# Transposing u by vector-engine block transposes and SBUF-to-SBUF copies in place of TensorE transposes

## The chip, the cores and the metric

One core of a Trainium2 chip. Times are microseconds of device time for one execution; the kernel before was timed three times. PE is TensorE, DVE VectorE, ACT ScalarE, POOL GpSimd and SP SyncE. DMAs issued from POOL go through the software queue, those from SP and ACT through hardware queues.

## The reference

A causal sliding-window attention (window 64) feeds a mixer block. B = 8, H = 8, S = 576, D = 64, so the model width is 512 and there are 4608 tokens.

```python
scores = scale * q @ k^T                  # masked to 0 <= i - j < 64
attn   = softmax(scores)                  # sum + 1e-9 in the denominator
x      = (attn @ v) as [B, S, H * D]
h      = x^T @ U @ V                      # rank 32, along the sequence
u      = x + h^T
out    = u + relu(u @ w_ch1) @ w_ch2      # 512 -> 2048 -> 512
```

## The kernel before

All matmuls are in bf16 and accumulate in f32. The weights are loaded once: `w1b` (512x2048) and `w2b` (2048x512).

The mixer's two large matmuls run over nine chunks of 512 tokens. The attention runs over eight batches of 576 tokens, so the borders of the two don't agree: tokens are counted in tiles of 128, `g` = 0 to 35, and chunk c is tiles 4c to 4c+3. Batch 0's attention is done ahead of everything (the prologue). From then on **stage c** is the mixer of chunk c with the attention of batch c+1 put in between its matmuls.

A stage has 32 slots. Slots 0 to 15 are `ch1(i)`: four matmuls of 512 columns into one bank (`psA`, L513) and a relu of it into `c1[i]`, on DVE for i = 1, 4, 7, 10, 13 and otherwise on ACT. Slots 16 to 31 are `ch2(t, quarter)`: four matmuls into `psU` (L535); after the fourth quarter DVE adds `u` (`osb`, L544) and SP stores the tile. `psA` and `psU` take turns in three banks of the pool `mm`. The loop at L655 runs each slot's matmuls and then the pieces of attention that the tables `PLACE`, `PLACE_1` (batch 1) and `PLACE_2` (batch 2) put behind that slot. The order of each engine's work is the order in which this loop writes it; every engine runs its own in that order.

The pieces of a batch b, with the engine that works longest in each:

- `KT` (L228): DVE transposes q and k in 32x32 blocks, from the loaded `kr`, `qr` into `kt`, `qt`. The KT of batch b+1 stands in the stage of batch b. For batches 0 to 2 ("paired") it moves pairs of bf16 as uint32, four instructions; from batch 3 on eight instructions of bf16.
- `S` (`SC`, L317): six pieces of scores on PE, exp on ACT (`pts`), the mask on DVE.
- `VC` (L263): DVE copies `vA` into `vB`, where the rows of v are shifted by 64.
- `PV` (L364): five tiles of attn @ v on PE, then a reciprocal and a multiplication on DVE, giving `xs`.
- `U` (L395): five matmuls into `pshh`, one copy on ACT (`hh`).
- `V` (L413): h^T on PE (`psv`) and the addition on DVE that gives `u` (`un`, one buffer for each tile g), for tiles (0,1), (2,3) and (4) of the batch.
- `UT` (L441): four PE transposes of a `u` tile by the identity (`tpu` or `tpw`, L451) and one copy out of PSUM (L456) into `uTc`, the operand of `psA`. Chunk 0 has another way (`XT` and `UP`, L469 and L481): x and h are multiplied by the identity and by V so that u comes out transposed.

`psA` contracts over the width in four parts of 128: part dc holds the features 128 dc to 128 dc + 127, of `uTc` and `w1b` alike.

Loads of q, k and v are all issued by POOL, in order. `load_kq(b)` fills `kr`, `qr` number b % 2. From batch 3 on it takes eight DMAs, one for each of four parts of k and of q in turn (k, q, k, q, ...), and loads each element twice, at two shifts. `load_v(b)` takes four DMAs into `vA` and one into `vB`, buffer b % 2. In stage c with b = c+1 the loop first issues `load_v(b + 1)` and, for b > 2, `load_kq(b + 2)`; in stage 1 `load_kq(4)` follows after slot 5, and in stage 0 `load_kq(2)` stands at the start and `load_kq(3)` after slot 23. They start as soon as their buffers are free.

Of the kernel before, what the change touches and what calls it, by code (L numbers as in the profile page):

```python
# [8 lines left out]
ACT = mybir.ActivationFunctionType  # L9
ALU = mybir.AluOpType  # L10

BF16 = mybir.dt.bfloat16
FP32 = mybir.dt.float32
# [3 lines left out]
def kernel(  # L17
# [43 lines left out]
    u_pool = ctx.enter_context(tc.tile_pool(name="un", bufs=14))  # L61
    c1_pool = ctx.enter_context(tc.tile_pool(name="c1", bufs=1))
    wk_pool = ctx.enter_context(tc.tile_pool(name="wk", bufs=2))
    out_pool = ctx.enter_context(tc.tile_pool(name="osb", bufs=4))
    ps_big = ctx.enter_context(tc.tile_pool(name="ps_big", bufs=2, space=bass.MemoryType.PSUM))
    first = ExitStack()
# [8 lines left out]
    NT = 5  # L75
    ident = const.tile([P, P], BF16, name="ident")
    mask = const.tile([P, 2 * NB, W], BF16, name="mask")
    w1b = const.tile([P, NDC, F], BF16, name="w1b")
    w2b = const.tile([P, NFC, DM], BF16, name="w2b")
    ub = [const.tile([P, NT, R], BF16, name=f"ub{i}") for i in range(2)]  # L80
    vrep = const.tile([P, W + S + W], BF16, name="vrep")
    bias = const.tile([P, 12, W], BF16, name="bias")
    idle = const.tile([P, CH], BF16, name="idle")
    xs = [const.tile([P, NT, H, D], BF16, name=f"xs{i}") for i in range(2)]
    vA = [const.tile([P, NFULL, H, VW], BF16, name=f"vA{i}") for i in range(2)]
# [102 lines left out]
    )  # L188
    nc.vector.tensor_copy(out=bias[:, NB:12, :], in_=bias[:, 6:NB, :])

    w1v = moe_w_ch1.rearrange("(c p) n -> p c n", p=P)
    w2v = moe_w_ch2.rearrange("(i p) m -> p i m", p=P)

    def load_w1(lo, hi):
        nc.gpsimd.dma_start(out=w1b[:, :, lo:hi], in_=w1v[:, :, lo:hi])

    def load_w2(lo, hi):
        nc.gpsimd.dma_start(out=w2b[:, lo:hi, :], in_=w2v[:, lo:hi, :])
# [11 lines left out]
    u_tiles = {}  # L210
    uT_tiles = {}

    def uT_of(c):
        if c not in uT_tiles:
            uT_tiles[c] = uT_pool.tile([P, NDC, CH], BF16, name="uTc")
        return uT_tiles[c]


    def attention(b, alone=False):
# [221 lines left out]
        def UT(t):  # L441
            def f():
                g = g0 + t
                wide = b == 1 and t % 2 == 1
                if wide:
                    tpb = ps_big.tile([P, 2, 2 * CH], BF16, name="tpw", tag="big")
                    tp = tpb[:, 0, 0:CH].rearrange("p (c q) -> p c q", q=P)
                else:
                    tp = psum["tp"].tile([P, NDC, P], BF16, name="tpu", tag="tp")
                for dc in range(NDC):  # L450
                    nc.tensor.transpose(  # L451
                        tp[:, dc, :], u_tiles[g][:, dc * P : (dc + 1) * P], ident[:]
                    )
                col = (g % TPC) * P
                copy = dve_copy if wide else nc.scalar.copy
                copy(out=uT_of(g // TPC)[:, :, col : col + P], in_=tp[:])  # L456
            return f

        pcs["KT"] = [KT(x, n) for n in range(NJ if pair else NJJ) for x in "kq"]
# [9 lines left out]
        def XT(t):  # L469
            def f():  # L470
                for dc in range(NDC):
                    nc.tensor.matmul(
                        xT0[dc // 2][:, dc % 2, t * P : (t + 1) * P],
                        x[:, t, 2 * dc : 2 * dc + 2, :].rearrange("p h d -> p (h d)"),
                        ident[:],
                        start=(t == 0),
                        stop=False,
                    )
            return f

        def UP():  # L481
            for dc in (0, 2, 1, 3):
                nc.tensor.matmul(
                    xT0[dc // 2][:, dc % 2, :],
                    hh["sb"][:, dc * P : (dc + 1) * P],
                    vrep[:, W : W + CH],
                    start=False,
                    stop=True,
                )
            for dc in (0, 2, 1, 3):  # L490
                copy = dve_copy if dc // 2 else nc.scalar.copy
                copy(out=uT_of(0)[:, dc, :], in_=xT0[dc // 2][:, dc % 2, :])  # L492

        pcs["XT"] = [XT(t) for t in range(NFULL)]
        pcs["UP"] = UP
        pcs["PV"] = [PV(t) for t in range(NT)]
        pcs["U"] = [UM((t,)) for t in range(NT)] if alone else [UM(tuple(range(NT)))]
        pcs["V"] = [VM((0, 1)), VM((2, 3)), VM((4,))]
        pcs["UT"] = [UT(t) for t in range(NT if odd else NT - 1)]
        return pcs  # L500


    DVE_RELU = (1, 4, 7, 10, 13)

    def mlp(c):
        uTc = uT_of(c)
        c1 = [None] * NFC

        def ch1(i):
            def f():  # L510
                ps = psum["mm"].tile([P, CH], FP32, name="psA", tag="mm")
                for dc in (0, 2, 1, 3) if c == 0 else range(NDC):
                    nc.tensor.matmul(  # L513
                        ps[:],
                        w1b[:, dc, i * P : (i + 1) * P],
                        uTc[:, dc, :],
                        start=(dc == 0),
                        stop=(dc == NDC - 1),
                    )
                c1[i] = c1_pool.tile([P, CH], BF16, name=f"c1_{i}")  # L520
                if i in DVE_RELU:
                    nc.vector.tensor_relu(out=c1[i][:], in_=ps[:])  # L522
                else:
                    nc.scalar.activation(out=c1[i][:], in_=ps[:], func=ACT.Relu)  # L524
            return f

        acc = {}

        def ch2(t, quarter):
            def f():  # L530
                g = c * TPC + t
                if quarter == 0:
                    acc[t] = psum["mm"].tile([P, DM], FP32, name="psU", tag="mm")
                for i in range(4 * quarter, 4 * quarter + 4):
                    nc.tensor.matmul(  # L535
                        acc[t][:],
                        c1[i][:, t * P : (t + 1) * P],
                        w2b[:, i, :],
                        start=(i == 0),
                        stop=(i == NFC - 1),  # L540
                    )
                if quarter == 3:
                    osb = out_pool.tile([P, DM], FP32, name="osb")
                    nc.vector.tensor_tensor(  # L544
                        out=osb[:], in0=acc[t][:], in1=u_tiles[g][:], op=ALU.add
                    )
                    nc.sync.dma_start(out=outf[g * P : (g + 1) * P, :], in_=osb[:])
            return f

        order = [(t, r) for t in range(TPC) for r in range(4)]  # L550
        if c == 0:
            order = [(t, r) for r in range(4) for t in range(3)] + [(3, r) for r in range(4)]
        return [ch1(i) for i in range(NFC)] + [ch2(t, r) for t, r in order]


    PLACE = {
        "VC": [0],
        "S": [1, 1, 4, 4, 7, 7],
        "PV": [10, 10, 13, 13, 15],
        "KT": [8, 9, 11, 12, 14, 15, 16, 18],  # L560
        "U": [17],
        "V": [19, 20, 22],
        "UT": [21, 22, 23, 24, 25],
    }
    PLACE_1 = {
        "KT": [13, 14, 15, 16],
        "S": [16, 16, 18, 18, 20, 20],
        "VC": [21],
        "PV": [23, 23, 25, 25, 26],
        "U": [28],  # L570
        "V": [29, 30, 31],
        "UT": [30, 31, 31, 32, 32],
    }
    PLACE_2 = {
        "KT": [1, 2, 3, 4],
        "S": [5, 5, 8, 8, 11, 11],
        "VC": [9],
        "PV": [14, 14, 16, 16, 18],
        "U": [20],
        "V": [22, 23, 24],  # L580
        "UT": [24, 25, 26, 27, 28],
    }
    KT_3 = [19, 20, 21, 23, 25, 27, 29, 30]
    KT_4 = [11, 12, 14, 16, 18, 19, 22, 25]


    def turn_over(n, cols=CH, to=None):
# [67 lines left out]
    for c in range(NCH):  # L655
        slots = [[] for _ in range(NSLOT + 1)]

        def place(b, parts, where):
            if b not in att:
                att[b] = attention(b)  # L660
            for part in parts:
                for f, s in zip(att[b][part], where[part]):
                    slots[s].append(f)

        b = c + 1
        if b == 1:
            for f, n in zip(att[0]["V"], (6, 8, 10)):
                slots[n].append(f)
        if b < B:
            if b == 1:  # L670
                load_kq(2)
            if b + 1 < B:
                load_v(b + 1)
            if b + 2 < B and b > 2:
                load_kq(b + 2)
            if b == 2:
                slots[5].append(lambda: load_kq(4))
            if b == 1:
                slots[23].append(lambda: load_kq(3))
            where = {1: PLACE_1, 2: PLACE_2}.get(b, PLACE)  # L680
            if b <= 2:
                place(b, ("KT",), where)
            place(b, ("VC", "S", "PV"), where)
            if 3 <= b + 1 < B:
                place(b + 1, ("KT",), {2: {"KT": KT_3}, 3: {"KT": KT_4}}.get(b, PLACE))
            place(b, ("U", "V", "UT"), where)
        for fill, extra in zip(mlp(c) + [lambda: None], slots):
            fill()
            for f in extra:
                f()  # L690
# [30 lines left out]
```

## Time and profile before

| | us |
|---|---|
| median of 3 runs (329.2 to 330.07) | 329.75 |
| the profiled execution | 330.28 |
| its span, first to last instruction | 328.6 |
| prologue, up to the first psA | 23.8 |
| stage 0, up to the first psA of stage 1 at 63.74 | 39.9 |
| stages 1 to 6, each | 33.98 to 34.80 |
| stage 7, without attention | 27.8 |
| stage 8, without attention, to the end of the span | 31.5 |
| busy in 132.8 to 166.8 (stage 3): PE, DVE, ACT, POOL | 34.0, 23.3, 13.7, 10.8 |

The groups of instructions that the change touches (each line: line, engine, operation, tiles, shape, count, then busy us, mean ns of one, idle us of the engine before them and what ended it):

```profile
L513 PE MATMUL psA<-uTc,w1b 128*128 128x512 bf16 x576 | 131.4, 379 | 0.9 <-DVE uTc L492 0.6
L456 ACT COPY uTc<-tpu 128x512 bf16<-128x512 bf16 x30 | 17.6, 586 | 40.3 <-PE tpu L451 40.3
L431 DVE TENSOR_TENSOR un<-psv,xs 128x512 bf16<-128x512 f32 (+1 forms) x40 | 25.7, 682 | 7.0 <-PE psv L420 6.8
```

The time of a psA matmul, 379 ns, is from its start to its modelled end; in stage 7, 64 of them follow each other in 13.81 us, one every 216 ns, so the sum of busy times is more than the time they take. ACT's 40 us before `uTc` are idle time of an engine with little to do at that point, not a cost. The granted TensorE clock was full (0.998) throughout.

The DMA rows of the page (busy share in 40 slices of 8.2 us, in tenths; and what was moved):

```profile
DMA  7999999999999997999991911001100010021011
GB/s 120 156 199 209 206 137 173 206 197 141 170 189 180 181 111 96 203 105 63 176 225 13 73 64 67 1 2 55 75 2 0 34 66 30 2 89 39 2 64 64
```

The DMA engines are at work almost all the time up to about 175 us, then in short stretches: by 190 us the last loads have landed and only outputs are left.

### The profile page before, as it was taken

How to read it: one execution, taken by the hardware profiler on the slowest of the kernel's cores; microseconds unless marked ns; L12 is line 12 of the kernel's file. 1: busy time of each engine (PE TensorE's matmuls, PEld its weight loads, DVE VectorE, ACT ScalarE, POOL GpSimd, SP SyncE). 2: the span in 40 equal slices, each digit the busy share in tenths (PEclk: the TensorE clock that was granted, in tenths of full speed). 3: DMA queues.
4: the chain of work that ended last, by engine and by line, in shares of the span. 5: the costliest groups of instructions: out<-in, count | busy, mean ns of one | idle time of the engine just before them, and what ended most of it. 6: DMA issues, size and time to landing. Idle time of an engine off the chain costs nothing.

```text
span 328.6 us, 6914 instructions
## 1 busy us (share of the span) xinstructions
PE 318.5 (97%) x2949; PEld 156.3 (48%) x2949; DVE 195.1 (59%) x339; ACT 118.3 (36%) x188; POOL 83.0 (25%) x112
## 2 busy tenths in 40 slices
PE   8989989899999999999999999999999999999995
PEld 8544444454454545454544454445445444444442
DVE  7654759588787885689457955696456512212211
ACT  1524350365027423552246233732182224203400
POOL 8571419554626226125501400000000000000000
PEclk9999999999999999999999999999999999999999
DMA  7999999999999997999991911001100010021011
GB/s 120 156 199 209 206 137 173 206 197 141 170 189 180 181 111 96 203 105 63 176 225 13 73 64 67 1 2 55 75 2 0 34 66 30 2 89 39 2 64 64
DMA packets 96573, 34.34 MB, mean 105 GB/s; under 512 B 86688, under 2 KB 89888, under 8 KB 96544
## 3 DMA queue, kind: packets, MB, share of 16 engines
q0 software_dynamic: 91360, 24.48, 83.8%
q1 hardware_dynamic: 5184, 9.44, 8.3%
q8 instruction: 23, 0.38, 0.5%
q14 instruction: 6, 0.05, 0.1%
HBM read 48.94 MB, written 9.44 MB: 178 GB/s over the span
## 4 chain that ended last, share of the span: by engine, by line
PE 79%; DMA 12%; DVE 5%; POOL 2%; issue 1%; ACT 0%; DVEq 0%
PE psU L535 36%; PE psA L513 32%; DMA vA<-in_v_dram 7%; DMA kr<-in_k_dram 5%; PE xr L375 3%; PE sc L341 3%; PE psv L420 2%; PE tpu L451 2%; PE pshh L401 1%; DVE un L431 1%; POOL vA L124 1%; DVE xs L385 1%; DVE kt L243 0%; DVE qt L243 0%; DVE osb L544 0%
## 5 line engine op out<-in xcount | busy, mean ns | idle before, releaser
L535 PE MATMUL psU<-w2b,c 128*128 128x512 bf16 x576 | 135.1, 379 | 0.0
L513 PE MATMUL psA<-uTc,w1b 128*128 128x512 bf16 x576 | 131.4, 379 | 0.9 <-DVE uTc L492 0.6
L524 ACT ACTIVATE c<-psA 128x512 bf16<-128x512 f32 x99 | 59.3, 599 | 100.2 <-PE psA L513 99.6
L513 PEld LDWEIGHTS <-w1b 128*128 128x128 bf16 x576 | 53.9, 98 | 63.9 <-issue 1.7
L535 PEld LDWEIGHTS <-c 128*128 128x128 bf16 x576 | 53.6, 98 | 60.2 <-issue 3.0
L544 DVE TENSOR_TENSOR osb<-psU,un 128x512 f32<-128x512 f32 x36 | 24.8, 690 | 64.0 <-PE psU L535 63.9
L522 DVE TENSOR_SCALAR c<-psA 128x512 bf16<-128x512 f32 x45 | 30.8, 685 | 34.8 <-PE psA L513 34.6
L124 POOL DMA_DIRECT2D vA<-in_v_dram x32 | 28.4, 892 | 62.2 <-PE xr L375 19.8
L349 ACT ACTIVATE pts<-sc 128x768 bf16<-128x768 f32 x42 | 31.8, 808 | 11.8 <-PE sc L341 10.0
L456 ACT COPY uTc<-tpu 128x512 bf16<-128x512 bf16 x30 | 17.6, 586 | 40.3 <-PE tpu L451 40.3
L356 DVE TENSOR_TENSOR pts<-pts,mask 128x768 bf16<-128x768 bf16 x42 | 23.1, 557 | 12.2 <-ACT pts L349 9.3
L431 DVE TENSOR_TENSOR un<-psv,xs 128x512 bf16<-128x512 f32 (+1 forms) x40 | 25.7, 682 | 7.0 <-PE psv L420 6.8
L385 DVE TENSOR_TENSOR xs<-xr,rcp 128x512 bf16<-128x512 f32 (+1 forms) x40 | 27.6, 691 | 1.4
L112 POOL DMA_DIRECT2D kr<-in_k_dram x20 | 16.6, 828 | 21.8 <-DVE kt L243 8.8
L375 PEld LDWEIGHTS <-pts 128*64 128x64 bf16 x576 | 12.4, 110 | 10.4 <-DVE xs L385 5.2
L112 POOL DMA_DIRECT2D qr<-in_q_dram x20 | 16.5, 826 | 3.0 <-DMA vA<-in_v_dram 1.1
L243 DVE STREAM_TRANSPOSE kt<-kr 128x576 bf16<-128x576 bf16 x20 | 16.0, 799 | 0.0
L243 DVE STREAM_TRANSPOSE qt<-qr 128x576 bf16<-128x576 bf16 x20 | 15.7, 787 | 0.0
L375 PE MATMUL xr<-vB,pts 128*64 128x65 bf16 x320 | 15.4, 196 | 0.3 <-DVE vB L137 0.2
L341 PEld LDWEIGHTS <-kt 64*64 64x64 bf16 (+1 forms) x720 | 10.1, 105 | 10.8 <-issue 10.4
L410 ACT CAST hh<-pshh 128x512 bf16<-128x512 f32 x8 | 4.7, 586 | 28.9 <-PE pshh L401 28.9
L341 PE MATMUL sc<-qt,kt 64*64 64x128 bf16 (+3 forms) x720 | 12.9, 215 | 1.8 <-issue 1.4
(64 smaller groups left out, 161.8 us busy)
## 6 DMA issues: line engine op xcount, KB each, us to landing
out_dram<-osb SPq DMA_DIRECT2D x36, 256.0 KB, 2.0
kr<-in_k_dram POOLq DMA_DIRECT2D x26, 288.0 KB, 10.4
qr<-in_q_dram POOLq DMA_DIRECT2D x26, 288.0 KB, 11.4
vA<-in_v_dram POOLq DMA_DIRECT2D x32, 128.0 KB, 7.2
w2b<-in_moe_w_ch_dram POOLq DMA_DIRECT2D x2, 1024.0 KB, 19.2
w1b<-in_moe_w_ch_dram POOLq DMA_DIRECT2D x2, 512.0 KB, 9.6
w1b<-in_moe_w_ch_dram POOLq DMA_DIRECT2D x1, 1024.0 KB, 10.6
vB<-in_v_dram POOLq DMA_DIRECT2D x8, 64.0 KB, 7.8
```

The costliest lines, as they stand in the source:

```text
L112: nc.gpsimd.dma_start(out=dst[32 * part : 32 * (part + 1), off : off + NJJ * RD].rearrange("p (n x) -> p n x", x=r * D), in_=src[b, m * NJ ...
L124: nc.gpsimd.dma_start(out=va[:, t, :, 0:D], in_=v[b, :, t * P : (t + 1) * P, :].rearrange("h p d -> p h d"),)
L243: nc.vector.transpose(out=dst[:, n * S : (n + 1) * S].rearrange("q (m p e) -> q m e p", p=32, e=r), in_=src[:, 32 + n * RD : 32 + (n + 1) ...
L341: nc.tensor.matmul(sc[half * W : (half + 1) * W, g, (a - lo) * W : (z - lo) * W], operand("k", g, jj, e, kb * W, (kb + 1) * W), operand("q ...
L349: nc.scalar.activation(out=dst, in_=sc[:, :, 0 : PB * W].rearrange("p g (n w) -> p g n w", w=W), func=ACT.Exp, scale=scale,)
L375: nc.tensor.matmul(xr[r0 : r0 + W, h // 4, (h % 4) * VW : (h % 4 + 1) * VW], pts[:, g, jj * NB + blk, :], rhs, start=True, stop=True,)
L385: nc.vector.tensor_tensor(out=x[lo:hi, t, :, :].rearrange("p (a h) d -> p a h d", a=2), in0=xv[:, :, :, 0:D], in1=rcp[lo:hi].to_broadcast( ...
L431: nc.vector.tensor_tensor(out=u_tiles[g][rs, :], in0=ps[rs, n, :], in1=xt[n][rs], op=ALU.add)
L513: nc.tensor.matmul(ps[:], w1b[:, dc, i * P : (i + 1) * P], uTc[:, dc, :], start=(dc == 0), stop=(dc == NDC - 1),)
L522: nc.vector.tensor_relu(out=c1[i][:], in_=ps[:])
L524: nc.scalar.activation(out=c1[i][:], in_=ps[:], func=ACT.Relu)
L535: nc.tensor.matmul(acc[t][:], c1[i][:, t * P : (t + 1) * P], w2b[:, i, :], start=(i == 0), stop=(i == NFC - 1),)
```

## The change

1. For chunks 2 to 8 the `UT` pieces are gone. In their place `TR(g)` transposes a `u` tile on DVE in 32x32 blocks of uint32, that is of pairs of neighbouring features, into a staging tile `stg` (two buffers), and `gather(c)` moves the blocks of the four tiles to their partitions with 16 DMAs inside SBUF, in turn from ACT and SP. Each moves 32 partitions of 1 KB in runs of 512 B. Chunk 1 keeps its `UT`, chunk 0 its own way.
2. So that pairs can stay together, the four parts of the contraction are now (g, e): features 256 g + 2 p + e on partition p. `w1b` is loaded in that order (each load as two DMAs), `uTc` holds the two features of a pair next to each other, and `psA` reads every second element of it. For chunks 2 to 8 the columns of `uTc` lie in the order (i, t, q), so `psA` reads them with three steps. `XT`, `UP` and chunk 1's `UT` take their columns with a step of two.
3. `next_loads(c)` takes the place of the early loads. It stands behind `gather(c + 1)` in stage c: two copies of one column on POOL that read what the last two DMAs of the gather wrote, then `load_v(c + 2)` and `load_kq(c + 3)`. The loads of stage 0 stay, `load_v(3)` and `load_kq(4)` move into stage 1's `next_loads`.
4. The tables move. From batch 3 on, S and PV come one or two slots earlier, VC goes from slot 0 to slot 3, KT starts at slot 12 in place of 8, U and V come two slots earlier. Batch 2's pieces come up to three slots earlier, batch 1's last ones about one.
5. `psA` of chunk 0's first two slots takes a buffer of the pool `ps_big`.

`TR` stands in the slots around the last `V` piece that chunk c+1 needs (`ready`): two transposes at `ready - 1`, one at `ready`, one at `ready + 1`, and there the gather and the loads. `ready` is 20 in stage 1, 18 in stage 2, 17 in stages 3 to 6 and 6 in stage 7.

```diff
-    w1v = moe_w_ch1.rearrange("(c p) n -> p c n", p=P)
+    w1v = moe_w_ch1.rearrange("(g p e) n -> g p e n", g=2, e=2)
...
-        nc.gpsimd.dma_start(out=w1b[:, :, lo:hi], in_=w1v[:, :, lo:hi])
+        for g in range(2):
+            nc.gpsimd.dma_start(out=w1b[:, g, :, lo:hi], in_=w1v[g, :, :, lo:hi])
...
+    def halves(ap):
+        return ap.rearrange("p (g q e) -> g e p q", g=2, e=2)
...
-            uT_tiles[c] = uT_pool.tile([P, NDC, CH], BF16, name="uTc")
+            uT_tiles[c] = uT_pool.tile([P, 2, CH, 2], BF16, name="uTc")
...
-        pcs["UT"] = [UT(t) for t in range(NT if odd else NT - 1)]
+        pcs["UT"] = [UT(t) for t in range(NT - 1)] if b == 1 else []
...
+    def TR(g):
+        def f():
+            c, t = divmod(g, TPC)
+            if c not in stages:
+                stages[c] = stg_pool.tile([P, 8, TPC, 32, 2], BF16, name="stg")
+            nc.vector.transpose(
+                out=stages[c][:, :, t, :, :].rearrange("p j q e -> p j (q e)").bitcast(U32),
+                in_=u_tiles[g].bitcast(U32).rearrange("p (j x) -> p j x", x=32),
+            )
+        return f
+
+    def next_loads(c):
+        def f():
+            for n in (14, 15):
+                i, j = (n + n // 4) % 4, n % 4
+                rows = slice(32 * j, 32 * (j + 1))
+                nc.gpsimd.tensor_copy(
+                    out=hold[rows, 0:1], in_=uT_of(c + 1)[rows, 0, i * TPC * 32, 0:1]
+                )
+            load_v(c + 2)
+            if c + 3 < B:
+                load_kq(c + 3)
+        return f
+
+    def gather(c):
+        def f():
+            run = TPC * 32
+            for n in range(16):
+                i, j = (n + n // 4) % 4, n % 4
+                queue = nc.sync if n % 2 else nc.scalar
+                queue.dma_start(
+                    out=uT_of(c)[32 * j : 32 * (j + 1), :, i * run : (i + 1) * run, :].rearrange(
+                        "p g n e -> p g (n e)"
+                    ),
+                    in_=stages[c][32 * i : 32 * (i + 1)].rearrange(
+                        "p (g j) t q e -> p g j (t q e)", g=2
+                    )[:, :, j, :],
+                )
+        return f
...
+                if c == 0 and i < 2:
+                    ps = ps_big.tile([P, 2, CH], FP32, name="psA0", tag="big")[:, 0, :]
+                else:
+                    ps = psum["mm"].tile([P, CH], FP32, name="psA", tag="mm")[:]
                 for dc in (0, 2, 1, 3) if c == 0 else range(NDC):
                     nc.tensor.matmul(
-                        ps[:],
-                        w1b[:, dc, i * P : (i + 1) * P],
-                        uTc[:, dc, :],
+                        ps if c < 2 else ps.rearrange("p (t i q) -> p t i q", i=4, t=TPC),
+                        w1b[:, dc // 2, dc % 2, i * P : (i + 1) * P],
+                        uT_cols(dc),
...
     PLACE = {
-        "VC": [0],
-        "S": [1, 1, 4, 4, 7, 7],
-        "PV": [10, 10, 13, 13, 15],
-        "KT": [8, 9, 11, 12, 14, 15, 16, 18],
-        "U": [17],
-        "V": [19, 20, 22],
-        "UT": [21, 22, 23, 24, 25],
+        "VC": [3],
+        "S": [0, 0, 3, 3, 6, 6],
+        "PV": [9, 9, 11, 11, 13],
+        "KT": [12, 13, 15, 16, 19, 21, 22, 24],
+        "U": [15],
+        "V": [17, 18, 20],
     }
...
     PLACE_1 = {
...
-        "S": [16, 16, 18, 18, 20, 20],
+        "S": [16, 16, 18, 18, 21, 21],
         "VC": [21],
         "PV": [23, 23, 25, 25, 26],
-        "U": [28],
-        "V": [29, 30, 31],
-        "UT": [30, 31, 31, 32, 32],
+        "U": [27],
+        "V": [28, 29, 31],
+        "UT": [29, 30, 31, 31],
     }
     PLACE_2 = {
-        "KT": [1, 2, 3, 4],
-        "S": [5, 5, 8, 8, 11, 11],
-        "VC": [9],
-        "PV": [14, 14, 16, 16, 18],
-        "U": [20],
-        "V": [22, 23, 24],
-        "UT": [24, 25, 26, 27, 28],
+        "KT": [0, 0, 1, 2],
+        "S": [2, 2, 5, 5, 8, 8],
+        "VC": [7],
+        "PV": [11, 11, 13, 13, 15],
+        "U": [17],
+        "V": [19, 20, 22],
     }
-    KT_3 = [19, 20, 21, 23, 25, 27, 29, 30]
-    KT_4 = [11, 12, 14, 16, 18, 19, 22, 25]
+    KT_3 = [16, 18, 19, 20, 24, 25, 27, 29]
...
             if b == 1:
                 load_kq(2)
-            if b + 1 < B:
-                load_v(b + 1)
-            if b + 2 < B and b > 2:
-                load_kq(b + 2)
-            if b == 2:
-                slots[5].append(lambda: load_kq(4))
-            if b == 1:
+                load_v(2)
                 slots[23].append(lambda: load_kq(3))
...
+        if 2 <= c + 1 < NCH:
+            g0 = (b * S) // P
+            first = (c + 1) * TPC
+            last = max(first + t - g0 for t in range(TPC)) // 2 if b < B else 0
+            ready = where["V"][last] if b < B else 6
+            for t in range(TPC):
+                slots[ready - 1 + t // 2 if t < TPC - 1 else ready + 1].append(TR(first + t))
+            slots[ready + 1].append(gather(c + 1))
+            if b + 1 < B:
+                slots[ready + 1].append(next_loads(c))
```

## The prediction

> **What bounds the kernel now.** I read the busy shares first, then the chain that ended last, then that chain inside one stage.
>
> ```profile
> PE 318.5 (97%) x2949; PEld 156.3 (48%) x2949; DVE 195.1 (59%) x339; ACT 118.3 (36%) x188; POOL 83.0 (25%) x112
> PE 79%; DMA 12%; DVE 5%; POOL 2%; issue 1%; ACT 0%; DVEq 0%
> ```
>
> PE is the bound. The DMA share of the chain lies in the prologue and stage 0. From 63.74 us (first psA of stage 1) to 324.72 us the chain is PE almost without a gap. Part of stage 3, from the chain in order of time (start, length, what):
>
> ```profile
> 156.23 0.86 PE psU L535 x4
> 157.09 0.22 PE tpu L451 x4
> 157.32 0.86 PE psU L535 x4
> 158.18 0.22 PE psv L420
> 158.40 0.22 PE tpu L451 x4
> ```
>
> Each UT tile (four transposes) is 0.22 us of PE, in line with the matmuls. First psA of each stage, from the same chain and the PE timeline: 63.74, 98.54, 132.69, 166.67, 201.13, 235.12, 269.27, 297.06. So stages 1 to 6 take 34.80, 34.15, 33.98, 34.46, 33.99 and 34.15 us, stage 7 27.8.
>
> **What is removed.** UT stays for the four tiles of chunk 1 only: 32 tiles become 4. 28 x 0.22 = 6.2 us of PE goes, all on the chain. With it go 28 uTc copies on ACT (586 ns each), which PE did not wait for outside stage 0's end. Stage 4 was 0.3 us longer than stage 2, which has as many tiles, in a stretch where the chain ran through DVE; I take that back too, since KT moves away from it. Stage lengths without UT: 33.9 for stage 1, 33.1 for 2 to 5.
>
> **Matmuls with a step of two.** psA now reads every second element. The score rows answer this, since the paired batches (32*64) already read with that step: a 64-column matmul takes 194 ns and a 192-column one 249 ns, exactly as for the unit-step batches (64*64). Equal slopes: I add nothing. From chunk 2 on the columns also jump after each run of 32, for which there is no row. Lower bound: nothing, and there is no reason for a gain. Upper bound: each run costs like a matmul of its own; 80 score matmuls take 3 x 0.46 us, 17 ns each, so 16 x 17 = 275 ns instead of 216 for a 512-column matmul, 59 ns x 64 x 7 = 26 us. I take nothing, because a jump inside one access is nearer to the single-instruction row.
>
> The other small edits (w1 in two loads, three more POOL issues of 0.78 us in the prologue, while loads are queued; psA0 in the big pool; the XT order; stage 0's slots) I take at 0, within -1 to +1: DVE uTc made psA wait 0.6 us once, and the three issues could cost up to 2.3 if that queue of loads were gone.
>
> **What is added on DVE.** 28 transposes of 128x256 uint32.
>
> ```profile
> L235 DVE STREAM_TRANSPOSE kt<-kr 128x576 uint32<-128x576 uint32 x6 | 7.5, 1248 | 0.9 <-DMA kr<-in_k_dram 0.9
> L243 DVE STREAM_TRANSPOSE kt<-kr 128x576 bf16<-128x576 bf16 x20 | 16.0, 799 | 0.0
> ```
>
> By the uint32 row 1248 x 256/576 = 0.55 us; by the bf16 row's rate 0.35; if a transpose cost the same at any size, 1.25. I take 0.55, same type and rate. Four per stage, 2.2 us, beside 23.3 us of DVE work in a stage of 34: no bound by itself, but they stand ahead of the copies, and with it ahead of the held loads. [...]
>
> **The copies.** 16 per chunk, 32 KB each, eight on SP, eight on ACT. The built order gives the HWDGE transfers eight completion semaphores in turn, so copies 8 to 15 each wait for the landing of the one eight before. The nearest row is the output store:
>
> ```profile
> L547 SPq DMA_DIRECT2D out_dram<-osb x36: 332/332/362, 53.9 to 325.4; - x36
> DMA to landing us min/median/max: 2.0/2.0/8.0
> ```
>
> Two queues: issue at 0, 0.33, 0.66, 1.0; the fourth lands at 3.0; its successor is issued then and lands at 5.0. Lower bound: issue time alone, 8 x 0.33 = 2.65. Upper bound: the loaded queue, where stores took 6.7 us (54.5 to 63): 1.0 + 2 x 6.7 = 14.4. I take 5.0, since the loads are held and the queue is empty. POOL's two one-column copies: two sub-microsecond instructions (MEMSET of one column 0.1, vB copies 0.6), I take 0.3 together.
>
> ACT is free when it issues these in stages 1 to 6 (no relu or exp in slots 17 to 31). **In stage 7 it isn't.** There they stand behind slot 7's work. In the trace of before DVE's relu of c_7 ends at 277.07; the last transpose ends at 277.6; ACT issues four, waits to 279.65, issues four until 280.98. Its next relu (c_8) began at 277.30 and now ends at 281.6. psA11, which takes c_8's bank (three banks), started at 269.43 + 11 x 0.863 = 278.92: PE stalls 2.7 us (2.3 with no landing time).
>
> **The held loads: the step that decides.** v(c+2) and k,q(c+3) now stand behind the copies on POOL; nothing but such loads queues there. Before, they were issued early: k,q of batch 5 from 97.46, read from 143.3 on. Cost of a batch, from the run at 153.86 with an otherwise empty queue:
>
> ```profile
> 153.86 0.82 POOL L112 DMA_DIRECT2D kr<-in_k_dram  x1 [2.57 <-DVE kt L243]
> 158.69 0.81 POOL L112 DMA_DIRECT2D kr<-in_k_dram  x1
> kr<-in_k_dram POOLq DMA_DIRECT2D x1, 288.0 KB, 13.0
> ```
>
> (The last line is the DMA view of the window around 158.7, from issue to landing.) The last k lands 158.69 + 13.0 - 153.86 = 17.8 us after the first issue. v goes first: 4 x 0.88 + 0.69 = 4.2 us of issue; vA has landed 6.5 us after it begins (2.65 to the fourth issue, 3.8 more by the load at 185.1). So k is complete **22.0 us after the loads begin**.
>
> When do they begin? Relative to the stage's start, with before's pieces (0.90 per ch1 slot between scores, 0.86 per ch2 slot, scores 0.46 per pair, PV 0.64 per pair, U 0.54, V 0.43), stages 3 and 4: V(0,1) ends at 20.4, U at 18.2; DVE has three KT and two of the new transposes until 20.5, then u, u, transpose, u, u, transpose (0.62 and 0.55 each) until 24.2. Plus 5.0 plus 0.3: 29.5. In stage 2 two transposes, a KT and an output add come between: 31.8. In stage 1 V comes later: 28.5 + 5.3 = 33.8.
>
> When are they needed? KT's first k stands at slot 12; DVE gets there, after PV(2) and PV(3), at 15.0 of the next stage. Behind it wait relu c_13 and the last xs, 2.3 us with KT itself, for which U (slot 15, PE at 17.6) waits. PE stalls by (k's landing - 15.3):
> - stage 2: 33.8 + 22.0 - 33.9 = 21.9, stall 6.6 (v lands at 6.4, asked for at 4.4; its stall is within this)
> - stage 3: 31.8 + 22.0 - 33.1 = 20.7, stall 5.4
> - stages 4 and 5: 29.5 + 22.0 - 33.1 = 18.4, stall 3.1 each
>
> Together 18.2 us. Stage 6 waits for no k; its v lands at 2.9. A stall moves the next loads and the next stage alike, so it is paid afresh in each stage.
>
> **Sum.** 328.6 - 6.2 - 0.3 + 2.7 + 18.2 = 343.0 us of span. The profiled run took 330.28, 1.7 over its span: 344.7. The median of the runs is 0.5 below it: 344.2, said as 344.
>
> Ends: copies at issue time alone take 2.35 from each of the four, leaving 8.8, and stage 7 pays 2.3: 334.5. Transposes at 0.35 take up to 0.8 more per stage: 331. Upwards, k delayed by v's tail (1 us), and 1 us of waits between copies and loads, times four: 352. Transposes at 1.25 would give 355; the loaded queue for the copies 37 us more; the jumps 26 more.
>
> **Rivals.**
> 1. The hold is hidden: k lands before DVE asks. For it: DVE works 23.3 of 34 us in a stage, so it has room to make up a late KT. Against it: c_13 and xs are behind KT in DVE's order, and even copies without landing time leave all four stages late. It decides if batch and copies together are 3 us faster than the rows in stages 4, 5 and 6 in 2. Then 328.6 - 6.5 + 2.7 = 324.8, median 326: faster.
> 2. The copies are slow, or PE slows on the runs of 32: the landing row spreads from 2.0 to 8.0, and no row has the jumps. Against it: the queue is empty by design, and the slopes are equal. Above 354.
> 3. Gains and stalls cancel: stalls of 4 us in all. Nothing sets it there: 330.
>
> **How the numbers follow.** Forecast 0.67, its own range 334 to 352; rival 1 0.17; rival 2 0.12; rival 3 0.04. The range 326 to 354 takes in the bounds but the highest and about half of rival 1. A difference of 0.3% (1 us) is what this kernel's measurement can tell from none: faster 0.17, same 0.03, slower 0.80.
>
> **What would show it.** Right: DVE idle before kt released by DMA kr in stages 2 to 5, shrinking from stage to stage; PE idle before pshh (U) of 3 to 7 us in each; PE idle before a psA in stage 7 of about 2.7 us, released by ACT; no tpu after stage 0. Steps wrong: copies landing in under 3 us; k landing less than 17 us after its first issue; psA above 379 ns from chunk 2 on. The forecast falls if stages 2 to 5 take 33 us each.

## The result, and the profile after

| | before | after |
|---|---|---|
| median, us | 329.91 (329.2 to 330.19, 4 runs) | 373.92 (372.21 to 375.6, 4 runs) |
| ratio of the times, 95% interval | | 1.1337, 1.1282 to 1.1393 |
| the profiled execution, its span | 330.28, 328.6 | 373.7, 371.5 |

Medians and ranges here take in all executions of a kernel, ratios only those within 1.5% of its fastest.

The change makes the kernel slower by 13%. The forecast was 344.0, and its range ended at 354: the sign was right, and the size was less than a third of what came (14 us of 44).

The busy shares of the page and its rows of PE and of the granted TensorE clock, of the kernel after:

```profile
PE 327.6 (88%) x2808; PEld 151.1 (41%) x2837; DVE 203.6 (55%) x367; ACT 101.8 (27%) x160; POOL 86.9 (23%) x125
...
PE   8899979899985899499988799599969999699995
...
PEclk9999989999996999989999999799999999699999
```

PE is no longer busy all the time: there are holes (4, 5, 6) where there was none after stage 0. And although the transposes by PE are gone, it is busy 9 us longer than before: behind some holes the clock row dips, and matmuls take longer there (psA 628 ns at a clock of 0.50 behind stage 3's hole, 387 at full clock, each to its modelled end); and each psA takes longer than before in every stage (from start to start 227 ns in place of 216, e7_layout, below). What PE waited for (engine and line, what it waited for, us in total, times, longest):

```profile
PE psA L575 <- DVE c L584: 20.5, 6, 5.0
PE pshh L407 <- DVE xs L391: 4.9, 5, 2.3
PE psA L575 <- ACT c L586: 3.2, 1, 3.2
PE psA L575 <- DMA out_dram<-osb: 1.9, 1, 1.9
```

The second line is the wait that was forecast at 18.2 us. The first is the large one. It is a relu on DVE that is late, and DVE's own list of waits says why (same columns):

```profile
DVE vB L138 <- DMA vA<-in_v_dram: 27.1, 8, 5.4
...
DVE kt L249 <- DMA kr<-in_k_dram: 6.1, 3, 3.0
```

DVE stands at `VC` (L138), waiting for v; the relu behind it in DVE's order can't run, its bank of `mm` isn't freed, and `psA` stops. The chain that ended last shows the whole loop from the copies of stage 2 to U of stage 3 (start us, length, what):

```profile
137.13 0.30 DVE stg L520
...
137.46 0.59 ACTq L547
...
141.99 1.91 DMA uTc<-stg
...
144.02 0.18 POOL hold L532
...
144.87 0.80 POOL vA L126
...
147.48 7.04 DMA vA<-in_v_dram
...
154.80 13.32 DMA kr<-in_k_dram
...
168.15 0.82 DVE kt L249
168.97 0.55 DVE c L584
...
169.66 0.69 DVE xs L391
...
170.40 0.38 PE pshh L407
```

From the last transpose (ended 137.43) to the first held load are 7.4 us, from there to v 9.7 (154.52), to the last k 23.3 (168.12). Stage 3 began at 144.75, so v came 9.8 us into it, where `VC` asked for it at 4.4.

The lower clock, in the windows behind that wait (window, its length, PE busy with psA of L575 and how many, granted clock, DMA share, GB/s):

```profile
157.00:158.00 1.00, 0.11 (x1) 0.79 2.71 153
158.00:159.00 1.00, 1.00 (x3) 0.50 2.96 161
159.00:160.00 1.00, 1.00 (x4) 0.50 2.78 152
160.00:161.00 1.00, 1.00 (x4) 0.50 2.83 155
161.00:162.00 1.00, 1.00 (x6) 1.00 2.21 174
```

PE resumed at 157.89, after 5.03 us; some 3.4 us, part of them still in the wait, went at half the clock. The stretches at half the clock are 3.41 us long in stages 0, 3 (157.59 to 161.00) and 6, and twice that, 6.83, in stages 2, 5 and 7. The length of the wait alone does not decide it, and the runs do not show what does: after 3.11 us in stage 4 (PE resumed at 196.83) the clock stayed full, and after 2.92 us in stage 6 (PE resumed at 276.54) it was halved for 3.41:

```profile
197.00:198.00 1.00, 1.00 (x6) 1.00 2.83 162
...
277.00:278.00 1.00, 1.00 (x4) 0.53 0.00 0
```

The lengths of the stages, from one first psA to the next (forecast: from the steps on record; the last two columns are experiments told of below):

| stage | before | forecast | after | e2_v_free | e12_k_first |
|---|---|---|---|---|---|
| prologue | 23.8 | 23.8 | 22.95 | 25.42 | 23.86 |
| 0 | 39.91 | 39.9 | 43.74 | 40.29 | 40.31 |
| 1 | 34.80 | 33.9 | 36.51 | 36.44 | 34.37 |
| 2 | 34.14 | 39.7 | 41.55 | 34.91 | 33.66 |
| 3 | 33.99 | 38.5 | 40.86 | 35.77 | 33.10 |
| 4 | 34.46 | 36.2 | 39.39 | 33.70 | 33.06 |
| 5 | 33.99 | 36.2 | 40.51 | 33.71 | 33.13 |
| 6 | 34.14 | 33.2 | 38.27 | 33.70 | 33.03 |
| 7 | 27.63 | 30.5 | 35.37 | 34.79 | 27.63 |
| 8 | 31.68 | 31.5 | 32.40 | 32.41 | 31.71 |

The first psA of stage 8 of the kernel before is at 296.89, not at the 297.06 that was on record; so its stages 7 and 8 are 27.63 and 31.68 us, not 27.8 and 31.5, and the 64 psA in 13.81 us are those of stage 8.

### The profile page after: what moved, and what is told of

It is laid out like the page before. It is cut to its first block, busy times and chain, and to the rows that moved or that the text cites. A ratio compares the mean times of both kernels' runs of the same rounds, so it can differ in the third digit from the quotient of the medians.

```text
span 371.5 us, 6830 instructions
## 1 busy us (share of the span) xinstructions
PE 327.6 (88%) x2808; PEld 151.1 (41%) x2837; DVE 203.6 (55%) x367; ACT 101.8 (27%) x160; POOL 86.9 (23%) x125
## 4 chain that ended last, share of the span: by engine, by line
DMA 34%; PE 32%; issue 16%; DVE 8%; POOL 6%; ACTq 3%; SPq 1%; POOLq 0%; ACT 0%; DVEq 0%
DMA vA<-in_v_dram 17%; PE psU L597 16%; PE psA L575 13%; DMA kr<-in_k_dram 11%; ACTq L547 3%; DMA w1b<-in_moe_w_ch_dram 3%; DMA uTc<-stg 2%; POOL vA L126 2%; DVE un L437 2%; DVE c L584 1%; PE psv L426 1%; PE xr L381 1%; POOL kr L114 1%; DVE kt L249 1%; POOL qr L114 1%
## 5 line engine op out<-in xcount | busy, mean ns | idle before, releaser
L575 PE MATMUL psA<-uTc,w1b 128*128 128x512 bf16 x571 | 148.5, 409 | 27.2 <-DVE c L584 20.5
L597 PE MATMUL psU<-w2b,c 128*128 128x512 bf16 x555 | 130.5, 382 | 1.3 <-issue 0.3
L575 PEld LDWEIGHTS <-w1b 128*128 128x128 bf16 x576 | 55.2, 100 | 102.4 <-issue 40.6
L597 PEld LDWEIGHTS <-c 128*128 128x128 bf16 x576 | 55.3, 98 | 73.9 <-issue 9.8
L532 POOL COPY hold<-uTc 32x1 bf16<-32x1 bf16 x10 | 1.8, 182 | 149.3 <-DMA uTc<-stg 148.8
L362 DVE TENSOR_TENSOR pts<-pts,mask 128x768 bf16<-128x768 bf16 x42 | 22.2, 553 | 14.4 <-ACT pts L355 13.1
L138 DVE COPY vB<-vA 64x2080 bf16<-64x2080 bf16 (+1 forms) x10 | 6.3, 629 | 27.1 <-DMA vA<-in_v_dram 27.1
L114 POOL DMA_DIRECT2D kr<-in_k_dram x20 | 17.4, 868 | 5.1 <-DMA vA<-in_v_dram 4.7
L114 POOL DMA_DIRECT2D qr<-in_q_dram x20 | 17.4, 868 | 1.7 <-DMA vA<-in_v_dram 1.3
L390 DVE RECIPROCAL rcp<-xr 128x8 f32<-128x8 f32 (+1 forms) x40 | 8.0, 201 | 14.3 <-PE xr L381 13.9
```

What stands on the lines that cost most here:

```text
L114: nc.gpsimd.dma_start(out=dst[32 * part : 32 * (part + 1), off : off + NJJ * RD].rearrange("p (n x) -> p n x", x=r * D), in_=src[b, m * NJ ...
L575: nc.tensor.matmul(ps if c < 2 else ps.rearrange("p (t i q) -> p t i q", i=4, t=TPC), w1b[:, dc // 2, dc % 2, i * P : (i + 1) * P], uT_col ...
L597: nc.tensor.matmul(acc[t][:], c1[i][:, t * P : (t + 1) * P], w2b[:, i, :], start=(i == 0), stop=(i == NFC - 1),)
```

## The experiments

The times of the kernel before beside these runs were 330.15 to 330.41 us.

**e1_no_hold** takes the hold out of the changed kernel.

```diff
         def f():
-            for n in (14, 15):
-                i, j = (n + n // 4) % 4, n % 4
-                rows = slice(32 * j, 32 * (j + 1))
-                nc.gpsimd.tensor_copy(
-                    out=hold[rows, 0:1], in_=uT_of(c + 1)[rows, 0, i * TPC * 32, 0:1]
-                )
             load_v(c + 2)
```

> The change without the hold: next_loads issues v and k,q without the two POOL copies that read the gather's last blocks, so the loads go out as soon as their buffers are free. Theory H (the held loads are what costs, v first): stages 2 to 6, now 38.3 to 41.6 us, fall to about 33.1 + 0.7 each; that takes some 31 us off the span of 371.5, so 340 (335 to 346). The copies then share the queue with k,q loads: they may land late and let PE wait a few us at a stage's start. Rival G (the copies, the psA access and the new DVE work cost by themselves): 365 or more.

362.78 us (360.21 to 365.26), ratio 1.0949 (1.0895 to 1.1002): a miss. The waits for v and k are gone, and stages 4 to 6 end at 33.69 to 33.71 us, but one wait took their place. PE's longest wait, and the chain through it:

```profile
PE psA L569 <- DMA uTc<-stg: 19.1, 2, 14.9
```

```profile
98.65 8.66 DMA uTc<-stg
...
107.33 8.85 DMA uTc<-stg
...
116.48 1.86 PE psA L569 x4
```

With loads under way the two copies of this chain land after 8.66 and 8.85 us in place of 1.9, and as copies 8 to 15 are issued only when the copy eight before has landed (here one lands at 107.31, and the next starts at 107.33), two such landings follow each other. Stage 2 began 14.94 us late, stage 3 4.17, and the granted clock was 0.958 over the span (psA behind the first wait up to 628 ns, to the modelled end). So the hold does something needed; the loads behind it are what costs.

**e2_v_free** leaves k and q held, and issues `load_v(c + 2)` at the start of stage c, ahead of that stage's copies and their hold.

```diff
                 )
-            load_v(c + 2)
             if c + 3 < B:
...
         b = c + 1
+        if 2 <= b and b + 1 < B:
+            load_v(b + 1)
```

> The change with v loaded early as before, at the start of a stage, and only k,q held. Theory H: the 5 us wait of DVE for v in each of stages 2 to 6 is gone, with the lower clock after it; k,q begin at the next stage's start, their last k lands 17.9 us into it where KT asks at 15.2, so 2 to 3 us of stall in stages 2 to 5: span near 350 (344 to 355). The recorded prediction's own step (the wait for k decides, v's is within it): no change from 371.

344.57 us (343.07 to 348.17), ratio 1.0439 (1.0369 to 1.051): 29 us less than the changed kernel, and its span of 341.1 lies below the 344 to 355 expected. No psA waits for `VC` any more. PE's waits for k, and for the copies of stages 7 and 1:

```profile
PE pshh L407 <- DVE xs L391: 3.8, 4, 1.9
PE psA L574 <- ACT c L585: 3.8, 1, 3.8
PE psA L574 <- DMA uTc<-stg: 1.7, 1, 1.7
```

The k wait is 1.04 us in stage 2, 1.90 in stage 3 and nothing in 4 and 5. The recorded stalls less the 4.2 us that v's issues no longer take are 2.4, 1.2 and below 0 twice.

**e6_kq_free** is the opposite: k and q early, v held.

```diff
             load_v(c + 2)
-            if c + 3 < B:
-                load_kq(c + 3)
...
+            if b == 2:
+                slots[5].append(lambda: load_kq(4))
+            if b + 2 < B and b > 2:
+                load_kq(b + 2)
```

> The counterpart: k,q loaded early as before, only v held. Theory H: v alone lands 6.5 us after its loads begin, about 6.5 us into the next stage where VC asks at 4.4: 2 us of stall in stages 2 to 6 and little or no lower clock: span near 350 (342 to 356). The recorded prediction's step (k decides): stalls nearly gone, 340 or less.

367.49 us (363.21 to 368.68), ratio 1.1074 (1.1 to 1.1147): a miss, and the counterpart of e2. PE still waits for relus behind `VC`, in each of stages 2 to 6:

```profile
PE psA L573 <- DVE c L582: 18.4, 6, 4.9
```

Holding v alone costs nearly as much as holding all.

**e3_relu_order** asks about the jumps. It is e1 with the columns of `uTc` read in order (still with a step of two), and the relu puts them back.

```diff
-            return cols.rearrange("p (i t q) -> p t i q", i=4, t=TPC)
+            return cols
...
+                dst, src = c1[i][:], ps
+                if c >= 2:
+                    dst = dst.rearrange("p (t i q) -> p i t q", i=4, t=TPC)
+                    src = src.rearrange("p (i t q) -> p i t q", i=4, t=TPC)
```

> No hold, and psA of chunks 2 to 8 reads uTc in its own column order, with a step of two only; the relu puts the columns back in token order as it writes c1. Theory A (the jumps after each run of 32 cost PE 11 ns in each psA matmul, 0.7 us in a chunk): about 5 us (3 to 6) less than e1, and 64 psA of stage 8 in 13.8 us in place of 14.5. Rival (the step of two costs, or the time is elsewhere): no change against e1. If ACT's or DVE's relu gets dearer by the strided access, stages with attention gain less than stage 8.

361.66 us (360.9 to 367.65), as the rival had it and not theory A. Stage 5 takes 33.67 us against 33.71 in e1, stage 8 32.39 against 32.41: the runs of 32 cost nothing.

**e7_layout** is the kernel before with the pair layout alone: w1 in pairs, `uTc` with the two features of a pair side by side, psA with a step of two. The PE transposes stay.

```diff
...
-            uT_tiles[c] = uT_pool.tile([P, NDC, CH], BF16, name="uTc")
+            uT_tiles[c] = uT_pool.tile([P, 2, CH, 2], BF16, name="uTc")
...
-                        w1b[:, dc, i * P : (i + 1) * P],
-                        uTc[:, dc, :],
+                        w1b[:, dc // 2, dc % 2, i * P : (i + 1) * P],
+                        uTc[:, dc // 2, :, dc % 2],
```

> The kernel before with nothing but the new operand layout: w1 in pair order, uTc with the two features of a pair side by side for all nine chunks, psA reading it with a step of two; u still transposed by PE, loads and tables as before. Theory S (the step of two costs PE 11 ns in each psA matmul, whatever the column order): 576 x 11 ns = 6.3 us more than before, span 334 to 337, 64 psA of stage 8 in 14.5 us. The recorded prediction took nothing for it: 328 to 330.

337.79 us (337.47 to 339.52), ratio 1.0236 (1.0198 to 1.0274). Each stage from 1 to 8 is 0.7 to 1.0 us longer, stage 0 2.3. The step has a price, and the timeline of PE shows it most cleanly in stage 8, with no attention. First the kernel before, then the changed kernel, then e12_k_first, which has no step (the 64 matmuls, and the first psU behind them):

```profile
296.89 13.98 PE L513 MATMUL psA<-uTc,w1b 128*128 128x512 bf16 x64
310.71 7.50 PE L535 MATMUL psU<-w2b,c 128*128 128x512 bf16 x34
```

```profile
339.15 14.67 PE L575 MATMUL psA<-uTc,w1b 128*128 128x512 bf16 x64
353.66 6.63 PE L597 MATMUL psU<-w2b,c 128*128 128x512 bf16 x29
```

```profile
292.14 13.98 PE L575 MATMUL psA<-uTc,w1b 128*128 128x512 bf16 x64
305.96 6.21 PE L597 MATMUL psU<-w2b,c 128*128 128x512 bf16 x28
```

From start to start 14.51 us in place of 13.82: 227 ns for a matmul, not 216. In e3 and e7, with the step and without the jumps, it is 14.50.

**e8_late7** is e2 with stage 7's transposes and copies moved from slot 6 to the second half of the stage, where ACT has no relu.

```diff
-            ready = where["V"][last] if b < B else 6
+            ready = where["V"][last] if b < B else 17
```

> e2 (v early, k,q held) with stage 7's transposes and gather around slot 17 in place of slot 6, where ACT has no relu left to do. Theory (stage 7 is 34.8 us long because ACT's relus stand behind its eight DMA issues, and because of the lower clock after that stall): stage 7 falls to 28.3, so the span to 334.5 (333 to 336). Rival (stage 7 is long for the gather's own traffic or DVE's transposes): 339 to 341.

340.13 us (339.21 to 344.75), ratio 1.0275 (1.0231 to 1.0318). Stage 7 fell from 34.79 to 28.32 us, as expected. The total is a miss: the profiled span fell from 341.1 to 338.4, not to 334.5. In this execution stages 1 and 5 took 1.5 and 1.2 us longer than in that of e2 (in stage 5 PE waited 1.05 us for k, in e2 not at all), and prologue and stage 0 together 0.7.

**e9_bf16_blocks** is e8 with DVE transposes of bf16 in place of pairs, so that `uTc` has its old layout and psA no step.

```diff
-                out=stages[c][:, :, t, :, :].rearrange("p j q e -> p j (q e)").bitcast(U32),
-                in_=u_tiles[g].bitcast(U32).rearrange("p (j x) -> p j x", x=32),
+                out=stages[c][:, :, t, :],
+                in_=u_tiles[g].rearrange("p (j x) -> p j x", x=32),
...
```

> e8 with DVE transposing 32x32 blocks of bf16 rather than of pairs: uTc and w1b get their old layout back and psA reads with a step of one. Theory S: 8 or 9 chunks x 0.6 to 0.7 us less than e8, while DVE's transposes take about 0.7 us each (rate of the bf16 KT row) in place of 0.41, which puts gathers some 1 us later: span 329 to 331, about the time of before. If the step isn't the cost, same as e8 or slower.

338.15 us (336.1 to 341.43), ratio 1.0215 (1.0159 to 1.0272): half a miss. Stages 6 to 8 fell to 33.03, 27.63 and 31.71 us. But k was late again, by 0.46, 2.44, 2.45 and 1.04 us in stages 2 to 5, and chunk 2's copies 2.82.

**e11_warm** asks what the lower clock costs. It is the changed kernel with matmuls whose result nobody reads, behind slot 6 of stages 2 to 6, to fill the wait.

```diff
+        if 2 <= c <= 6:
+            def warm():
+                ps = psum["tp"].tile([P, 2 * P], FP32, name="warm", tag="tp")
+                for _ in range(32):
+                    nc.tensor.matmul(
+                        ps[:], idle[:, 0:P], idle[:, 0 : 2 * P], start=True, stop=True
+                    )
+            slots[6].append(warm)
```

> The change as it is, with 32 matmuls of 256 idle columns (3.4 us) put on PE behind slot 6's scores in stages 2 to 6, where PE would wait for relu c_4 behind DVE's wait for v. Their result is unread. Theory W (after a wait of 4 to 5 us PE runs at half clock for 3.4 or 6.8 us): the low clock in stages 2, 3, 5 and 6 goes, 5 to 9 us less: span 362 to 367. Rival (the low clock costs nothing, PE waits anyway): no change, or slower by what the idle matmuls take beyond the wait.

370.5 us (369.21 to 372.45), ratio 1.122 (1.1171 to 1.127), 3.4 us below the changed kernel; its span of 367.1 is at the upper end of the 362 to 367 expected. Of the 4.5 us between the two profiled spans 2.5 lie in stages 0 and 7, which have none of these matmuls; stages 2 to 6 together are 1.9 us shorter. The granted clock over the span was 0.991, in the changed kernel 0.959. In stage 2 it fell behind the later wait for k. In stages 3, 5 and 6 it stayed full, and the stages are 0.9 and 1.1 us shorter in 5 and 6 and no shorter in 3 (41.01 us), where the next wait took it up:

```profile
PE pshh L407 <- DVE xs L391: 7.8, 6, 2.5
PE psA L575 <- DVE c L584: 3.6, 4, 1.4
```

The wait for k, 4.9 us in the changed kernel, is 7.8 here. The slow matmuls ahead of it were paid for, at least in part, by that wait.

**e12_k_first** and **e13_k_first_pairs** make what was left early enough: of a batch the four loads of k go first and the four transposes of k first, and in stage 1 U and V come earlier and KT of batch 3 later. e12 does this to e9, e13 to e8.

```diff
+        pairs = [(p, x) for p in range(n) for x in "kq"]
+        if not PAIRED[b]:
+            pairs = [(p, x) for x in "kq" for p in range(n)]
...
-        pcs["KT"] = [KT(x, n) for n in range(NJ if pair else NJJ) for x in "kq"]
+        if pair:
+            pcs["KT"] = [KT(x, n) for n in range(NJ) for x in "kq"]
+        else:
+            pcs["KT"] = [KT(x, n) for x in "kq" for n in range(NJJ)]
...
-        "U": [17],
-        "V": [19, 20, 22],
+        "U": [16],
+        "V": [17, 18, 21],
     }
-    KT_3 = [16, 18, 19, 20, 24, 25, 27, 29]
+    KT_3 = [21, 22, 23, 24, 25, 27, 28, 29]
```

> e9_bf16_blocks with the four loads of a batch's k ahead of the four of q (before: k, q, k, q), the four transposes of k ahead of those of q, and in stage 1 U one slot and V one or two slots earlier, with KT of batch 3 behind the transposes of u. No part of the computation changes. If what is left in e9 is only lateness (k landing behind four loads of q, and the copies for chunk 2 issued at 94.5 us, 2.82 us too late), it goes: four issues of 0.81 us and the transfers behind them are taken from ahead of the last k, about 6 us, where the waits were 0.46 to 2.45; q is asked for some 6 us after k. Stages 2 to 5 fall to 33.0 to 33.3 us each, stage 1 to about 34.6, and the time is 324 to 328, below the kernel before (329.9). Rival: the waits only move, to q or to v, or the lower clock comes from something else; then stages 2 to 5 stay at 34 to 37 and the time at 335 to 338.

> The same three moves in e8_late7, so with the transposes of pairs (0.41 us a tile in place of 0.68) and psA with a step of two. If the moves take the waits away here too, what stands between this kernel and e12_k_first is the price of the step of two less nothing: 0.7 us a stage in stages 1 to 8, some 5 to 6 us, so 329 to 334. Rival: the cheaper transposes matter, since the copies and the loads start 1 us earlier in each stage; then it comes within 2 us of e12_k_first.

e12: 325.22 us (324.73 to 325.72), ratio 0.9843 (0.9813 to 0.9874): 1.6% less than the kernel before, a gain that is clear of the spread of the runs but under 2%. e13: 332.02 us (330.5 to 334.94, 10 runs), ratio 1.0062 (1.0031 to 1.0093). The busy shares and rows of PE and of the clock of e12, and two of its waits of PE, those for k and for the copies:

```profile
PE 312.8 (97%) x2837; PEld 150.4 (46%) x2837; DVE 209.0 (65%) x367; ACT 101.2 (31%) x160; POOL 85.7 (26%) x122
...
PE   8889989899999999999999999999999999999995
...
PEclk9999999999999999999999999999999999999999
```

```profile
PE pshh L410 <- DVE xs L394: 0.9, 2, 0.5
...
PE psA L575 <- DMA uTc<-stg: 0.5, 1, 0.5
```

No hole is left after stage 0, and PE has 5.7 us less to do than before (318.5), the UT tiles. Stages 2 to 6 take 33.03 to 33.66 us in e12, 33.70 in e13: the step of two is all that parts them there, and the cheaper transposes of pairs bring nothing once nothing waits for them. Which of the three moves did how much was not tried apart.

## Why the prediction was wrong

**Right.** Without waits and without the step, stages 3 to 6 take 33.03 to 33.13 us in e12, where the forecast had 33.1 for 2 to 5: the UT tiles were worth what the chain showed. The held loads decide, DVE waits for k ahead of `kt`, and k was complete 23.3 us after the loads began, forecast at 22.0. The jumps cost nothing. The transposes were cheaper than taken:

```profile
L520 DVE STREAM_TRANSPOSE stg<-un x28: 380/416/435, 92.4 to 311.8; 128x256 uint32<-128x256 uint32 x28
```

0.42 us (minimum, median, maximum in ns; then the first and last start), not 0.55, and a third of the 1.25 that the prediction gave for a cost that is the same at any size.

**The step that failed: v.** "vA has landed 6.5 us after it begins" and, for stage 2, "v lands at 6.4, asked for at 4.4; its stall is within this", for stage 6 "its v lands at 2.9". The 3.8 us for the last landing came from a load at 185.1 that had been issued 2 us behind the one before it; from stage 3 on the kernel before let its v loads go one or two at a time, as the readers of their buffer finished. Released together they are issued every 0.89 us, and the later a load was issued, the longer it took to land: 4.2, 5.5, 6.0 and 7.0 us for stage 3, 3.8, 5.0, 5.6 and 6.8 for stage 6. From issue to landing (minimum, median, maximum) of the four loads that stage 3 waits for, and of those that stage 6 waits for, behind which no k or q was issued:

```profile
DMA to landing us min/median/max: 4.2/5.8/7.0
```

```profile
DMA to landing us min/median/max: 3.8/5.3/6.8
```

The last of four takes 6.8 to 7.0 us: 9.4 to 9.7 after the loads begin. As stage 6 has it with no k or q behind them, these aren't what it takes (output stores were in flight beside them). The trace of before had one such case, the four v loads from 50.19 to 53.01, issued together in stage 0 with k and q under way:

```profile
DMA to landing us min/median/max: 6.0/6.2/7.3
```

In stage 6 v landed 7.8 us in (273.31 less 265.51), not at 2.9: 2.9 us of the difference are the landing, 9.4 for 6.5, and 2.0 the later start of the loads (the copies, below). And the wait isn't "within" that for k: both are in DVE's order, so the earlier one is paid first and only the rest of the later one behind it. PE's idle time in stages 2 to 6:

| | 2 | 3 | 4 | 5 | 6 | sum |
|---|---|---|---|---|---|---|
| forecast, k | 6.6 | 5.4 | 3.1 | 3.1 | 0 | 18.2 |
| measured, behind v | 4.40 | 5.03 | 3.11 | 4.20 | 2.92 | 19.7 |
| measured, behind k | 1.21 | 0.45 | 2.35 | 0 | 0 | 4.0 |

e2 and e6 show the same from both sides: v out of the hold takes 29 us off, k and q out of it 6. In total the idle time is only 5.5 us more than forecast; what the steps left out stands around it:

- **The clock** had no term. By the granted shares, 3.41 us of full clock were lost in each of stages 2, 5 and 7, 1.71 in stages 0, 3 and 6: 15.4 in all (the mean over the span was 0.959). e11 shows that it is worth less than its sum: with the clock at 0.991 the wait for k grew from 4.9 to 7.8 us, and stages 2 to 6 together became only 1.9 us shorter.
- **The step of two**, "equal slopes: I add nothing", taken from matmuls of 64 and 192 columns (why these show no cost is open): a psA takes 227 ns, not 216, 5% more, which is 0.7 us a stage, 5.6 us for stages 1 to 8.
- **The copies.** 5.0 us with issues of 0.33; with POOL's copies 5.3 from the last transpose to the first load. Landing was 1.9 us as expected, but an issue of these copies holds ACT and SP for 0.61, not the output store's 0.33: 6.8 for the copies and 0.7 for POOL's in stage 2, 7.4 to 7.8 in all in stages 1 to 5. It puts the loads 2 us later in every stage.
- **Stage 7**, "2.7 us": the place and the mechanism were right, the size not. Eight issues took ACT from 312.36 to 318.24, the relu of c_8 began at 318.34, and psA resumed at 318.98, 4.0 us of idle time (0.78 and 3.21) and 3.4 of clock. (The 2.3 for no landing time is about 1.9 by the forecast's own rows: eight issues of 0.33 and a relu of 0.6 from 277.6 on, against 278.92.)

```profile
312.36 5.88 ACTq L547 DMA_DIRECT2D uTc<-stg  x8
318.34 1.57 ACT L586 ACTIVATE c<-psA 128x512 bf16<-128x512 f32 x3 [7.35 <-DMA uTc<-stg]
```

- **Stage 1's copies** came 1.9 us after PE was ready for chunk 2 (the wait that the list puts down to `out_dram`; POOL's hold copies, which read the landed data, began at 102.95 and psA at 103.20).
- **The small edits**, "within -1 to +1": stage 0 took 3.8 us more, 1.7 of them by the clock, the prologue 0.9 less, so that stage 1 began at 66.69, not 63.74. In the nine runs with the pair layout it begins at 64.6 to 66.7, in e9 and e12 without it at 64.6 and 64.2. How much of this is the layout, and by what part of it, is open; copies into `uTc` with a step take ACT 730 ns, not 586.

Against the 28.5 us that the span is above its forecast, these are 5.5 for the waits, 15.4 for the clock at most, 5.6 for the step, 1.3 for stage 7's idle time, 1.9 for chunk 2's copies and 1.2 for the rest of prologue and stage 0: 30.9. The 2.4 too much are counted twice: 5.0 us of the stretches at half the clock lie inside waits, before PE resumed, so 2.5 of the 15.4 are already in the idle time.

The time fell among those of rival 2 (above 354), but not by its mechanism: the copies landed fast (1.9 us, median) and the runs of 32 cost nothing (stage 5 took 33.71 us with them in e1, 33.67 without in e3). Rivals 1 and 3 fell with the waits themselves.

## What to carry to other kernels

Here a v load landed after 3.8 us when it was issued 2 us behind the one before it, and after 6.8 to 7.0 as the last of four issued every 0.89: before loads are released together, price the last of them, not a lone one, and the first that is asked for before the longest. A wait that holds loads back for a transfer's sake should hold only those that can afford it, in the order in which they are needed; here v out of the hold, k ahead of q, U and V of stage 1 earlier, the copies away from a busy ACT and a layout without a step turned 13% of loss into 1.6% of gain. When a forecast says that PE will wait for some us, the slower clock behind the wait needs a term of its own: here nothing to 3.4 us behind waits of 2 to 5 us, less where a later wait takes it up.

## What the runs showed of the hardware

- A copy inside SBUF of 32 partitions with two runs of 512 B each holds the issuing queue for 0.61 us, an output store of 256 KB for 0.33.
- Copies inside SBUF land in 1.9 us (median) with the loads held and in 6.8 to 10.2 with loads under way (chunk 2 of e1_no_hold).
- Behind waits of PE in the changed kernel the granted clock was halved for 3.41 us (stages 0, 3 and 6) or 6.83 (2, 5 and 7): after two of 1.52 and 0.70 us in stage 0 and after one of 2.92 in stage 6, not after one of 3.11 in stage 4.
- A 512-column bf16 matmul whose moving operand has a step of two takes 227 ns, not 216; jumps after each 32 columns add nothing (stage 5 of e1_no_hold with them 33.71 us, of e3_relu_order without them 33.67).
- A DVE transpose in 32x32 blocks of 128x512 bf16 takes 0.68 us (0.69 median in e12), the same bytes as uint32 pairs 0.42.
